# Softmax sums kept in one tile, range-checked in pieces, with a general version behind a branch

## The chip, the cores and the metric

The kernel runs on one core of a Trainium2 chip. The metric is the device time of one launch in microseconds (us), median of several runs. The core has five engines that work through queues of their own: TensorE (PE in the profile, its weight loads PEld), VectorE (DVE), ScalarE (ACT), GpSimd (POOL) and SyncE (SP), and 16 DMA engines.

## The reference

A dynamic convolution over 7 taps, whose weights are a softmax, followed by a two-layer network with the nonlinearity h - tanh(h). Shapes: x is 8 x 4096 x 192, weight_gen is 8 x 4096 x 8 heads x 7 taps, the two matrices are 192 x 2048 and 2048 x 192, all float32.

```python
def _attn_ref(x, weight_gen):
    B, S, D = x.shape
    H, K = (weight_gen.shape[2], weight_gen.shape[3])
    group = D // H
    w = weight_gen - np.max(weight_gen, axis=-1, keepdims=True)
    w = np.exp(w)
    w = w / (np.sum(w, axis=-1, keepdims=True) + 1e-09)
    pad = K - 1
    x_pad = np.concatenate([np.zeros((B, pad, D), dtype=np.float32), x], axis=1)
    idx = np.arange(S)[:, None] + np.arange(K)[None, :]
    x_unf = x_pad[:, idx, :].copy().reshape(B, S, K, H, group)
    return np.einsum('bshk,bskhg->bshg', w, x_unf).reshape(B, S, D)

def _moe_ref(x, w_in, w_out):
    h = x @ w_in
    g = h - np.tanh(h)
    return (g @ w_out).astype(np.float32)
```

The inputs of the softmax are normal numbers times 0.3. The reference subtracts the maximum of the 7 taps before the exponential.

## The kernel before

The 32768 tokens are cut into 32 blocks (n = 0 to 31) of 1024 tokens, 128 partitions with 8 tokens each. The whole loop over blocks is written out, and within `manual_schedule` (L564) the order of the Python calls is the order of the instructions in each engine's queue. No planner reorders them.

For a block the work is this. SP loads weight_gen (`load_wg`) and x with a halo of 6 rows (`load_x`). ScalarE takes the exponential in place (`softmax_exp`, L169), without subtracting a maximum. VectorE sums over the 7 taps (`softmax_sum`, L183, two halves of 128x224 elements to 128x32 in most blocks, into a tile `zsum` from a pool), takes the reciprocal (`softmax_norm`, L198, written to a corner of a PSUM tile) and scales (L229). GpSimd multiplies x by the weights, tap by tap (`products`, L299); transfers that add (L236) and transposing matmuls into one PSUM tile (`conv_sums`, L384) sum the taps; ScalarE copies the result to SBUF as bf16 (`conv_out`, L410). VectorE does the first two taps of one or two tokens of some blocks in a step of another block (`help`, L250 and L251).

The network runs in 16 steps f of 128 hidden units. `gemm1(n, f)` (L427) multiplies into a PSUM tile `ph` of 128x1024 float32, six matmuls; ScalarE takes tanh (L440), VectorE subtracts and writes a bf16 tile `gt` (L441). The second matmul (L495) is written as a stream of pairs, `out_pairs(m)`, that are laid between the steps: while block n runs its 16 steps, the pairs belong to block n-1, and a table (`STEADY` for the late blocks: 5, 11, 0, 16, 4, 12, ... pairs behind step 0, 1, 2, ...) says how many stand behind which step. The last pair of each group of 16 reads the `gt` of step 15. For block 31 the second matmul is done at the end, in `gemm2_last` (L538, L551, L552, L554): matmul, copy on ScalarE, add on VectorE, and a store on SP for every two of eight parts.

The tiles `ph` and the PSUM tiles of the transposes come from one pool, `psum_h`, with three buffers. So a step's matmul waits until the subtraction of the tile three places earlier has read it. The transposes for the next block stand behind steps 13 and 14 (`t2`, `t1`); block 31 has none. Where there is a later softmax, its reciprocal and scaling come behind step 14 (`softmax_norm`, "scale"). Blocks 28 to 31 have no later softmax: `soft` names block n+4 and is empty there.

The loop of blocks, with the places that the change touches:

```python
    for n in range(1, NTOT):
        ...
        soft = [m for m in (n + 3 if n <= AHEAD else n + 4,) if m < NTOT]
        for f in range(NFT):
            ph = gemm1(n, f)
            ...
            if n > 1:
                for h, at in enumerate(plan["sums"]):
                    if soft and f == at:
                        softmax_sum(soft[0], h * JH, (h + 1) * JH)
```

At the program's end each engine jumps to a last block, SP waits for all transfers, and all engines meet at two barriers, between which GpSimd clears the semaphores (all of it on line L800).

Of the kernel before, what the change touches and what calls it, by code (L numbers as in the profile page):

```python
# [8 lines left out]
FP32 = mybir.dt.float32  # L9
BF16 = mybir.dt.bfloat16  # L10

ACT = mybir.ActivationFunctionType
AX = mybir.AxisListType


@with_exitstack
def kernel(
# [8 lines left out]
    nc = tc.nc  # L26

    B, S, D = x.shape
    H, K = weight_gen.shape[2], weight_gen.shape[3]
    G = D // H  # L30
    F = moe_w_in.shape[1]
    P = nc.NUM_PARTITIONS
    R = P // 2
    HALO = K - 1

    J = 8
    TOK = P * J
    JH = J // 2
    HT = TOK // 2
    NSB = S // TOK  # L40
    NTOT = B * NSB
    NFT = F // P
    NC = D // R
# [7 lines left out]
    HELP = {n: ((n - 2, 3),) for n in (4, 5, 6, 7, 8, 9, 10, 11, 12, 13, 14, 15, 16, 17, 18, 19, 20, 21, 22, 23, 24, 25, 26, 27, 28, 29, 30, 31)} | {9: ((7, 3), (6, 12)), 10: ((8, 3), (7, 12)), 11: ((9, 3), (8, 12)), 12: ((10, 3), (9, 12)), 13: ((11, 3), (10, 12)), 14: ((12, 3), (11, 12))}  # L51
    LAST_TAP = (4, 5, 6, 7, 8)
    X_LATE = ()
    ZERO_AT = 8
    PACE, PACED = None, ()
    SCALE_TWICE = True
# [24 lines left out]
    zero = const.tile([1, D], FP32, name="zero")  # L81
    nc.vector.memzero(zero[:])
    once = const.tile([P, 1], FP32, name="once")

    x_of = {}
    held = {}
# [2 lines left out]
    zsum_of = {}  # L89
    zr_of = {}  # L90
    wsm_of = {}
    prods_of = {}
    to_sum = {}
    conv_of = {}
    g_of = {}
# [71 lines left out]
    def softmax_exp(n):  # L167
        wg_t = wg_of.pop(n)
        last_exp[0] = nc.scalar.activation(  # L169
            out=wg_t[:].rearrange("p j h k -> p (j h k)"),  # L170
            in_=wg_t[:].rearrange("p j h k -> p (j h k)"),
            func=ACT.Exp,
        )
        e_of[n] = wg_t
# [4 lines left out]
    def softmax_sum(n, j0=0, j1=J):  # L179

        if j0 == 0:
            zsum_of[n] = wgpool.tile([P, J * H], FP32, name="zsum")
        nc.vector.reduce_sum(  # L183
            out=zsum_of[n][:, j0 * H : j1 * H],
            in_=e_of[n][:, j0:j1].rearrange("p j h k -> p (j h) k"),
            axis=AX.X,
        )

    def softmax_recip(n, j0=0, j1=J):
        if j0 == 0:  # L190
# [3 lines left out]
    def softmax_norm(n, bank):  # L194

        wsm = softmax_tile()
        zr_v = bank[:, 512 - J * H : 512]
        nc.vector.reciprocal(zr_v, zsum_of[n][:])  # L198

        def finish():  # L200
            scale(nc.vector, wsm[:], e_of[n], zr_v)

        wsm_of[n] = (wsm, None, None, None)
        return finish

    def softmax_norm_ramp(n, bank):

        softmax_sum(n)
        wsm = softmax_tile()
        zr_v = bank[:, 512 - J * H : 512]  # L210
        nc.vector.reciprocal(zr_v, zsum_of[n][:])  # L211
        if n == 2:
            scale(nc.vector, wsm[:], e_of[n], zr_v)
            wsm_of[n] = (wsm, None, None, None)
            return
        wsm_v = bank[:, 0 : J * H * K].rearrange("p (j h k) -> p j h k", j=J, h=H)
        if n == 0 and SCALE_TWICE:
            scale(nc.vector, wsm[:], e_of[n], zr_v)
        ramp_scale[n] = scale(nc.vector, wsm_v, e_of[n], zr_v)
        if n == 1 or not SCALE_TWICE:  # L220
            nc.scalar.activation(  # L221
                out=wsm[:].rearrange("p j h k -> p (j h k)"),
                in_=wsm_v.rearrange("p j h k -> p (j h k)"),
                func=ACT.Copy,
            )
        wsm_of[n] = (wsm, wsm_v, None, None)
# [302 lines left out]
    def gemm2_last(j, f0=0, f1=NFT):  # L529

        n = NTOT - 1
        if f0 == 0:
            half[j] = psum_h.tile([P, 2, HT], FP32, name="po2", tag="ph")
        po = half[j]
        col = (j % 2) * HT + (j // 2) * P
        for f in range(f0, f1):
            for r in range(2):
                nc.tensor.matmul(  # L538
                    po[:, r, 0:D],
                    lhsT=g_of[n][f][r * R : (r + 1) * R, col : col + P],  # L540
                    rhs=w_out[r * R : (r + 1) * R, f, :],
                    start=(f == 0),
                    stop=(f == NFT - 1),
                )
# [15 lines left out]

    w_in = const.tile([P, NC, F], BF16, name="w_in")
    w_out = const.tile([P, NFT, D], BF16, name="w_out")

    ctx.enter_context(tc.manual_schedule())  # L564

    def load_w_out():
        nc.gpsimd.dma_start(out=w_out[:], in_=moe_w_out.rearrange("(c p) e -> p c e", c=NFT))
# [139 lines left out]
    for n in range(1, NTOT):  # L707
        more = n < NTOT - 1
        finish = []
        plan = FIRST if n == 1 else DOUBLE if n in DOUBLE_IN else APART if n in APART_IN else STEADY  # L710
# [4 lines that stand above are left out]
            if n == 1:  # L715
                if f == 1:
                    load_wg(5)
                if f == 5:
                    softmax_exp(4)
                steps = ((softmax_sum, 3), (softmax_recip, 3), (softmax_sum, 4))  # L720
                for at, (step, m, h) in zip(plan["sums"], [s + (h,) for s in steps for h in (0, 1)]):
                    if f == at:
                        step(m, h * JH, (h + 1) * JH)
                if f == 5:
                    wsm_of[3] = (softmax_tile(), None, e_of[3], zr_of[3])
                    rest = products(3)
            elif f == 1:
                if soft:
                    softmax_exp(soft[0])
                if n + 2 < NTOT:  # L730
                    rest = products(n + 2)
            if n == AHEAD and f == 4:
                softmax_exp(n + 4)
            if n > 1:
                for h, at in enumerate(plan["sums"]):
                    if soft and f == at:
                        softmax_sum(soft[0], h * JH, (h + 1) * JH)
            if n == AHEAD:
# [33 lines left out]
    gemm2_last(0, J, NFT)  # L772
    for j in range(1, J):
        gemm2_last(j)


# [28 lines left out]
```

## Time and profile before

| | |
|---|---|
| runs | 746.22 us median of 3 (744.88 to 746.73) |
| the profiled execution, span from first to last instruction | 743.4 us |
| TensorE busy | 722.3 us (97%) |
| VectorE busy | 687.4 us (92%) |
| ScalarE busy | 638.8 us (86%) |
| GpSimd busy | 654.5 us (88%) |
| L441, subtraction, 512 times | 601.6 us, 1217 ns each |
| L440, tanh, 512 times | 512.1 us, 1025 ns each |
| L183, sums, 61 times | 23.6 us |
| L198, reciprocals, 27 times | 14.9 us, 550 ns each |
| L229, scaling on VectorE, 27 times | 16.8 us, 621 ns each |
| granted TensorE clock | 0.995 of full |

Busy times are shares of one span in which the engines overlap. The span is that of one profiled execution; the runs' times cover what lies around it, too. In the prediction's extracts a timeline row has a start (us), a duration (us), the engine, the line, the operation with its result and its operands, a count, and in brackets the idle time before and what ended it. Rows that follow each other on an engine and are alike are put together, and their duration runs from the first start to the last end.

### The profile page before, as it was taken

To read this page: it belongs to the slowest core of one execution; us is meant where nothing else is said; L and a number is where in the kernel's file an instruction comes from. 1 tells how busy PE (TensorE), PEld (TensorE's weight loads), DVE (VectorE), ACT (ScalarE), POOL (GpSimd) and SP (SyncE) were. 2 spreads that over 40 slices of the span, in tenths; PEclk is the share of its full clock that TensorE was granted. 3 is DMA by queue.
4 is the path that set the end of the run, shared out by engine and by line. 5 is a ranking of instruction groups with operands and counts; after the bars stand their busy time and mean duration, and the time that the engine had idled before them with its cause. 6 is when DMAs were issued, how large, how long until landed. Compare 5 with 4: busy or idle time off the path is not lost.

```text
span 743.4 us, 30037 instructions
## 1 busy us (share of the span) xinstructions
PE 722.3 (97%) x13616; PEld 556.5 (75%) x13616; DVE 687.4 (92%) x723; ACT 638.8 (86%) x872; POOL 654.5 (88%) x163
## 2 busy tenths in 40 slices
PE   3899999999999999999999999999999999999997
PEld 2477777778777777777777777777777777877777
DVE  7999899999999999999999999999999999988893
ACT  4888888888888888989889999898998989888882
POOL 7999999999999999999999999999999999991000
PEclk9899999999999999999999999999999999999999
DMA  8925367766567668878777977877887877776112
GB/s 236 245 46 161 135 172 185 195 179 149 124 183 184 183 185 224 210 199 203 166 202 209 236 186 204 178 195 205 221 209 195 192 181 194 193 149 110 45 45 86
DMA packets 34269, 130.06 MB, mean 175 GB/s; under 512 B 4591, under 2 KB 9439, under 8 KB 30174
## 3 DMA queue, kind: packets, MB, share of 16 engines
q0 software_dynamic: 19424, 51.12, 40.4%
q1 hardware_dynamic: 14718, 77.03, 27.6%
q8 instruction: 106, 1.74, 0.9%
q14 instruction: 21, 0.17, 0.1%
HBM read 54.52 MB, written 25.17 MB: 107 GB/s over the span
## 4 chain that ended last, share of the span: by engine, by line
PE 92%; DVE 5%; ACT 1%; issue 1%; DMA 1%; SPq 0%; DVEq 0%
PE ph L427 43%; PE obank L495 43%; PE pc L384 4%; DVE gt L441 3%; PE po L538 1%; ACT th L440 1%; DVE pa L299 1%; DMA wg_t<-in_weight_gen_dram 1%; DVE zsum L183 0%; SPq L134 0%; ACT convT L402 0%; DVE obank L211 0%; DVE pa L251 0%; DVE pb L299 0%; SPq L144 0%
## 5 line engine op out<-in xcount | busy, mean ns | idle before, releaser
L441 DVE TENSOR_TENSOR gt<-ph,th 128x1024 bf16<-128x1024 f32 x512 | 601.6, 1217 | 33.4 <-ACT th L440 23.2
L440 ACT ACTIVATE th<-ph 128x1024 f32<-128x1024 f32 x512 | 512.1, 1025 | 69.2 <-PE ph L427 60.3
L427 PE MATMUL ph<-convT,w_in 64*128 64x512 bf16 x3072 | 415.1, 379 | 5.3 <-DVE gt L441 3.3
L495 PEld LDWEIGHTS <-gt 64*128 64x128 bf16 x7936 | 355.6, 94 | 80.6 <-issue 6.3
L495 PE MATMUL obank<-w_out,gt 64*128 64x192 bf16 x7936 | 408.0, 243 | 0.9 <-issue 0.8
L299 POOL TENSOR_TENSOR pa<-x_t,wsm 128x2688 bf16<-128x2688 f32 (+3 forms) x68 | 338.9, 5232 | 0.2
L299 POOL TENSOR_TENSOR pb<-x_t,wsm 128x4608 bf16<-128x4608 f32 (+2 forms) x33 | 283.8, 8601 | 0.7 <-ACT wsm L221 0.5
L427 PEld LDWEIGHTS <-w_in 64*128 64x128 bf16 x3072 | 163.0, 94 | 86.0 <-issue 18.3
L514 ACT ACTIVATE out_sb<-obank 128x192 f32<-128x192 f32 x248 | 81.3, 328 | 11.2 <-PE obank L495 10.3
L410 ACT ACTIVATE convT<-pc 128x1024 bf16<-128x1024 f32 (+1 forms) x62 | 50.1, 810 | 2.9 <-PE pc L384 2.7
L236 POOL DMA_DIRECT2D pa<-pb x28 | 36.0, 1284 | 13.7 <-POOL pb L299 9.1
L384 PEld LDWEIGHTS <-pa 64*128 64x128 bf16 x2064 | 41.5, 100 | 6.8 <-DVE pa L299 1.1
L236 POOL DMA_DIRECT2D pa<-pa x21 | 34.7, 1651 | 9.6 <-DMA pa<-pb 8.9
L384 PE MATMUL pc<-ident,pa 64*128 64x64 bf16 x1968 | 41.2, 191 | 1.8 <-POOL pa L299 0.9
L183 DVE TENSOR_REDUCE zsum<-wg_t 128x32 f32<-128x224 f32 (+1 forms) x61 | 23.6, 387 | 2.9 <-ACT wg_t L169 2.9
L169 ACT ACTIVATE wg_t<-wg_t 128x448 f32<-128x448 f32 x32 | 18.2, 570 | 6.3 <-DMA wg_t<-in_weight_gen_dram 6.2
L251 DVE TENSOR_TENSOR pa<-x_t,ph 128x384 bf16<-128x384 f32 x34 | 18.8, 554 | 2.0 <-DVE ph L250 0.3
L229 DVE TENSOR_TENSOR wsm<-wg_t,pc 128x448 f32<-128x448 f32 x27 | 16.8, 621 | 2.5
L198 DVE RECIPROCAL pc<-zsum 128x64 f32<-128x64 f32 x27 | 14.9, 550 | 0.0
L384 PE MATMUL pc<-ident,pb 64*128 64x64 bf16 x216 | 4.9, 206 | 9.0 <-POOL pb L299 9.0
L384 PEld LDWEIGHTS <-pb 64*128 64x128 bf16 x288 | 6.3, 106 | 9.5 <-POOL pb L299 9.0
L538 PE MATMUL po<-w_out,gt 64*128 64x192 bf16 x256 | 11.2, 243 | 0.0
(27 smaller groups left out, 56.8 us busy)
## 6 DMA issues: line engine op xcount, KB each, us to landing
x_t<-in_x_dram SPq DMA_DIRECT2D x31, 1344.0 KB, 7.9
pa<-pb POOLq DMA_DIRECT2D x28, 1152.0 KB, 9.5
out_dram<-out_sb SPq DMA_DIRECT2D x31, 768.0 KB, 3.9
pa<-pa POOLq DMA_DIRECT2D x21, 768.0 KB, 7.2
wg_t<-in_weight_gen_dram SPq DMA_DIRECT2D x32, 224.0 KB, 7.1
x_t<-in_x_dram SPq DMA_DIRECT2D x1, 768.0 KB
w_out<-in_moe_w_out_dram POOLq DMA_DIRECT2D x1, 768.0 KB, 9.5
out_dram<-out_sb SPq DMA_DIRECT2D x4, 192.0 KB, 3.0
```

The source lines that it names most:

```text
L183: nc.vector.reduce_sum(out=zsum_of[n][:, j0 * H : j1 * H], in_=e_of[n][:, j0:j1].rearrange("p j h k -> p (j h) k"), axis=AX.X,)
L236: return nc.gpsimd.dma_start(out=out.rearrange("p k j d -> p k (j d)"), in_=in_.rearrange("p k j d -> p k (j d)"), accum_op=mybir.AluOpTyp ...
L251: nc.vector.tensor_mul(pa[:, 0:KH, j, :].rearrange("p k (h g) -> p k h g", h=H), bass.AP(tensor=x_v.tensor, offset=x_v.offset + j * D, ap= ...
L299: return eng.tensor_mul(prod(k0, k1)[:, :, j0:j1].rearrange("p k j (h g) -> p k (j h) g", h=H), bass.AP(tensor=x_v.tensor, offset=x_v.offs ...
L384: nc.tensor.matmul(pc[r][:, col : col + R] if home else pc[:, r, col : col + R], lhsT=prods[c][gi][r * R : (r + 1) * R, 2 * j : 2 * j + 2] ...
L410: last_conv[0] = nc.scalar.activation(out=out, in_=pc[:, :, 0:cols].rearrange("p r (cj t) -> p r cj t", t=R), func=ACT.Copy,)
L427: nc.tensor.matmul(ph[:, r, :], lhsT=w_in[r * R : (r + 1) * R, c, f * P : (f + 1) * P], rhs=convT[r * R : (r + 1) * R, c, :], start=(c == ...
L440: last_act[0] = nc.scalar.activation(out=th[:], in_=ph_f, func=ACT.Tanh)
L441: last_sub[0] = nc.vector.tensor_sub(gt[:], ph_f, th[:])
L495: mm = nc.tensor.matmul(po[:, 0:D], lhsT=g_of[n][f][r * R : (r + 1) * R, col : col + P], rhs=w_out[r * R : (r + 1) * R, f, :], start=(r == ...
L514: last_act[0] = nc.scalar.activation(out=out_sb[:, j, :], in_=po[:, 0:D], func=ACT.Copy)
L538: nc.tensor.matmul(po[:, r, 0:D], lhsT=g_of[n][f][r * R : (r + 1) * R, col : col + P], rhs=w_out[r * R : (r + 1) * R, f, :], start=(f == 0 ...
```

## The change

The sums of exponentials of all 32 blocks go into one tile `zall` (128 x 2048) in place of a rotating tile per block. Eight pieces, at fixed places in the last four blocks, check that all sums lie between 1e-18 and 1e30: pieces 0 and 1 take the maximum over each half of `zall` per partition, 2 and 3 the minimum, 4 and 5 compare with the bounds, 6 multiplies the results and sends 128 x 2 numbers as one row to one partition through SP's queue, and 7 takes the minimum of that row into an integer `flag`. Behind the last block every engine reads `flag` into a register (`values_load`) and branches. If a sum was out of range, a loop over the 8 batches computes everything anew with the row maximum subtracted (`general`); otherwise that code is jumped over.

In the built program, up to the branch, each engine's instructions stand in the order of before, with the new ones between. SP's read of `flag` stands behind the transfer of the row and ahead of the last store of block 30 and the four stores of block 31. SP has four register moves more ahead of the first barrier. The engines' last block holds, for SP, a wait for each of the semaphores of transfers and engines; the way past the general version has some waits and updates of semaphores of its own. TensorE's part of the loop's body has 3,011 instructions, that of ScalarE 211, of VectorE 180, of SP some fifty.

```diff
@@ constants
+    SUM_MAX, SUM_MIN = 1e30, 1e-18
+    CHECK = {(28, 14): (0,), (29, 14): (1,), (30, 14): (2,), (31, 4): (3,), (31, 6): (4, 5, 6), (31, 13): (7,)}
@@ tiles
+    zall = const.tile([P, NTOT * J * H], FP32, name="zall")
+    ends = const.tile([P, 4], FP32, name="ends")
+    fine = const.tile([P, 2], FP32, name="fine")
+    fine_row = const.tile([1, 2 * P], FP32, name="fine_row")
+    flag = const.tile([1, 1], mybir.dt.int32, name="flag")
@@ softmax_sum
-            zsum_of[n] = wgpool.tile([P, J * H], FP32, name="zsum")
+            zsum_of[n] = zall[:, n * J * H : (n + 1) * J * H]
@@
+    def sums_piece(i):
+
+        w = NTOT * J * H // 2
+        if i < 4:
+            op = ALU.max if i < 2 else ALU.min
+            nc.vector.tensor_reduce(ends[:, i : i + 1], zall[:, i % 2 * w : (i % 2 + 1) * w], AX.X, op)
+        elif i == 4:
+            nc.vector.tensor_scalar(ends[:, 0:2], ends[:, 0:2], SUM_MAX, None, op0=ALU.is_le)
+        elif i == 5:
+            nc.vector.tensor_scalar(ends[:, 2:4], ends[:, 2:4], SUM_MIN, None, op0=ALU.is_ge)
+        elif i == 6:
+            nc.vector.tensor_mul(fine[:], ends[:, 0:2], ends[:, 2:4])
+            nc.sync.dma_start(out=fine_row[:], in_=fine[:])
+        else:
+            nc.vector.tensor_reduce(flag[:], fine_row[:], AX.X, ALU.min)
@@ softmax_norm, softmax_norm_ramp
-        nc.vector.reciprocal(zr_v, zsum_of[n][:])
+        nc.vector.reciprocal(zr_v, zsum_of[n])
@@
-    ctx.enter_context(tc.manual_schedule())
+    sched = tc.manual_schedule()
+    sched.__enter__()
@@ the loop of blocks, behind gemm1 and the loads of a step
+            for piece in CHECK.get((n, f), ()):
+                sums_piece(piece)
@@ the end
     for j in range(1, J):
         gemm2_last(j)
+    sched.__exit__(None, None, None)
+
+    def general(b, s):
+        ...
+        nc.vector.tensor_reduce(zr[:], e_v, AX.X, ALU.max)
+        nc.vector.tensor_sub(e_v, e_v, spread(zr[:]))
+        nc.scalar.activation(
+            out=e_t[:].rearrange("p j h k -> p (j h k)"),
+            in_=e_t[:].rearrange("p j h k -> p (j h k)"),
+            func=ACT.Exp,
+        )
+        ...
+
+    good = nc.values_load(flag[:], min_val=0, max_val=1)
+    with tc.If(good < 1, preferred_fallthrough_block=False):
+        with tc.For_i(0, B) as b:
+            for s in range(NSB):
+                general(b, s)
+            for s in range(NSB):
+                g_of.pop(NTOT + s)
+                conv_of.pop(NTOT + s)
```

More of the change, by code (lines that the diff above doesn't have):

```diff
@@ L13 @@
 AX = mybir.AxisListType
+ALU = mybir.AluOpType
 @with_exitstack
@@ L210, in softmax_norm_ramp @@
         zr_v = bank[:, 512 - J * H : 512]
-        nc.vector.reciprocal(zr_v, zsum_of[n][:])
+        nc.vector.reciprocal(zr_v, zsum_of[n])
         if n == 2:
@@ L774, with rows, spread @@
         gemm2_last(j)
+    sched.__exit__(None, None, None)
+    def general(b, s):
+        n = NTOT + s
+        s0 = s * TOK
+        x_t = xpool.tile([P, HALO + J, D], FP32, name="x_t")
+        def rows(p0, p1, r0, r1):
+            batch = x[bass.ds(b, 1)]
+            nc.sync.dma_start(
+                out=x_t[p0:p1, r0:r1, :],
+                in_=bass.AP(
+                    tensor=batch.tensor,
+                    offset=batch.offset + (s0 + p0 * J - HALO + r0) * D,
+                    ap=[[J * D, p1 - p0], [D, r1 - r0], [1, D]],
+                ),
+            )
+        if s == 0:
+            rows(0, P, HALO, HALO + J)
+            rows(1, P, 0, HALO)
+            nc.vector.memset(x_t[0:1, 0:HALO, :], 0.0)
+        else:
+            rows(0, P, 0, HALO + J)
+        e_t = wgpool.tile([P, J, H, K], FP32, name="wg_t")
+        nc.sync.dma_start(
+            out=e_t[:],
+            in_=weight_gen[bass.ds(b, 1), s0 : s0 + TOK].rearrange("o (p j) h k -> p (o j) h k", p=P),
+        )
+        e_v = e_t[:].rearrange("p j h k -> p (j h) k")
+        zr = wgpool.tile([P, J * H], FP32, name="zr")
+        def spread(v):
+            return v.rearrange("p (n o) -> p n o", o=1).to_broadcast([P, J * H, K])
+        nc.vector.tensor_reduce(zr[:], e_v, AX.X, ALU.max)
[4 more added lines that the diff above has]
+            func=ACT.Exp,
+        )
+        nc.vector.reduce_sum(out=zr[:], in_=e_v, axis=AX.X)
+        nc.vector.reciprocal(zr[:], zr[:])
+        nc.vector.tensor_mul(e_v, e_v, spread(zr[:]))
+        total = opool.tile([P, J, D], FP32, name="out_sb")
+        part = opool.tile([P, J, D], FP32, name="out_sb")
+        summed = pbpool.tile([P, J, D], BF16, name="pb")
+        x_v = x_t[:]
+        for k in range(K):
+            to = total if k == 0 else part
+            nc.vector.tensor_mul(
+                to[:].rearrange("p j (h g) -> p (j h) g", h=H),
+                bass.AP(tensor=x_v.tensor, offset=x_v.offset + k * D, ap=[x_v.ap[0], [G, J * H], [1, G]]),
+                e_t[:].rearrange("p j h (k o) -> p k (j h) o", o=1)[:, k].to_broadcast([P, J * H, G]),
+            )
+            if k > 0:
+                nc.vector.tensor_add((summed if k == K - 1 else total)[:], total[:], part[:])
+        prods_of[n] = [[summed[:]]] * NC
+        conv(n, (0, 1), (2,))
+        for f in range(NFT):
+            gemm1(n, f)
+        out_sb = opool.tile([P, J, D], FP32, name="out_sb")
+        for j in range(J):
+            po = psum_h.tile([P, 2, HT], FP32, name="po2", tag="ph")
+            col = (j % 2) * HT + (j // 2) * P
+            for f in range(NFT):
+                for r in range(2):
+                    nc.tensor.matmul(
+                        po[:, r, 0:D],
+                        lhsT=g_of[n][f][r * R : (r + 1) * R, col : col + P],
+                        rhs=w_out[r * R : (r + 1) * R, f, :],
+                        start=(f == 0),
+                        stop=(f == NFT - 1),
+                    )
+            ot = tpool.tile([P, D], FP32, name="ot", tag="th")
+            nc.scalar.activation(out=ot[:], in_=po[:, 0, 0:D], func=ACT.Copy)
+            nc.vector.tensor_add(out_sb[:, j, :], po[:, 1, 0:D], ot[:])
+        nc.sync.dma_start(
+            out=out.rearrange("(b s p j) e -> b s p j e", b=B, s=NSB, p=P)[bass.ds(b, 1), s].rearrange(
+                "o p j e -> p (o j) e"
+            ),
+            in_=out_sb[:],
+        )
```

## The prediction

> **What bounds the kernel now.** I read the share of each engine first, then the chain of work that ended last, then the timelines of VectorE and TensorE in the blocks where the new instructions stand, and last the instructions of the program's end.
>
> ```profile
> PE 722.3 (97%) x13616; PEld 556.5 (75%) x13616; DVE 687.4 (92%) x723; ACT 638.8 (86%) x872; POOL 654.5 (88%) x163
> ...
> PE 92%; DVE 5%; ACT 1%; issue 1%; DMA 1%; SPq 0%; DVEq 0%
> ```
>
> TensorE (PE) is busy for 97% of the span and makes 92% of the chain. VectorE (DVE) is close behind, so extra VectorE work costs time only where it makes TensorE wait. It does so through the ring of three PSUM tiles (psum_h): step f may write its tile only when the subtraction (L441) of the step three tiles earlier has ended.
>
> Blocks 27 and 28 on VectorE, around step 14 (start, duration, idle before in brackets):
>
> ```profile
> 640.01 0.55 DVE L198 RECIPROCAL pc<-zsum 128x64 f32<-128x64 f32 x1
> 640.66 0.62 DVE L229 TENSOR_TENSOR wsm<-wg_t,pc 128x448 f32<-128x448 f32 x1
> 641.20 3.67 DVE L441 TENSOR_TENSOR gt<-ph,th 128x1024 bf16<-128x1024 f32 x3
> ...
> 660.85 1.22 DVE L441 TENSOR_TENSOR gt<-ph,th 128x1024 bf16<-128x1024 f32 x1 [0.69 <-ACT th L440]
> 662.47 1.23 DVE L441 TENSOR_TENSOR gt<-ph,th 128x1024 bf16<-128x1024 f32 x1 [0.40 <-ACT th L440]
> 664.35 2.36 DVE L441 TENSOR_TENSOR gt<-ph,th 128x1024 bf16<-128x1024 f32 x2 [0.66 <-PE ph L427]
> ```
>
> Block 27 has a reciprocal and a scaling between the subtractions of steps 14 and 15; block 28 has none (there is no later softmax), and VectorE idles 0.40 and 0.66 us there. Now block 31. Its subtractions come in the groups f0-1, f2-3, f4-5 (at 713.26), f6-7 (715.87) and f8 to f13 (718.49); the first matmuls of TensorE below are those of f8 and f9, then f10 and f11 alone:
>
> ```profile
> 713.26 2.36 DVE L441 TENSOR_TENSOR gt<-ph,th 128x1024 bf16<-128x1024 f32 x2 [0.26 <-ACT th L440]
> 715.87 2.37 DVE L441 TENSOR_TENSOR gt<-ph,th 128x1024 bf16<-128x1024 f32 x2 [0.26 <-ACT th L440]
> 718.49 7.18 DVE L441 TENSOR_TENSOR gt<-ph,th 128x1024 bf16<-128x1024 f32 x6 [0.25 <-ACT th L440]
> ```
>
> ```profile
> 716.57 1.48 PE L427 MATMUL ph<-convT,w_in 64*128 64x512 bf16 x12
> 717.86 0.68 PE L495 MATMUL obank<-w_out,gt 64*128 64x192 bf16 x12
> 718.36 0.83 PE L427 MATMUL ph<-convT,w_in 64*128 64x512 bf16 x6
> ...
> 719.83 0.83 PE L427 MATMUL ph<-convT,w_in 64*128 64x512 bf16 x6
> ```
>
> What the reader is to see: the ring is tight here. Step 9 starts at 716.57 + 0.65 = 717.22 (six matmuls follow the next six by 0.65 us in the chain) and needs the subtraction of f6, which ends at 715.87 + 1.22 = 717.09: 0.13 us to spare. Step 10 starts at 718.36 and needs f7, which ends at 718.24: 0.12 us to spare. Step 8 (716.57) needs f5 (715.62): 0.95 us.
>
> Last, the prices of VectorE reductions, and the program's end (duration ns min/median/max, first and last start):
>
> ```profile
> L183 DVE TENSOR_REDUCE zsum<-wg_t 128x32 f32<-128x224 f32 x58 | 21.8, 375 | 0.0
> ...
> L183 DVE TENSOR_REDUCE zsum<-wg_t 128x64 f32<-128x448 f32 x3 | 1.8, 614 | 2.9 <-ACT wg_t L169 2.9
> ```
>
> ```profile
> L800 SPq EVENT_SEMAPHORE  x11: 17/28/28, 740.7 to 743.3; - x11
> ...
> L800 PEldq DRAIN  x2: 13/554/1095, 738.5 to 742.8; - x2
> ...
> L800 DVEq DRAIN  x2: 19/207/395, 740.0 to 742.8; - x2
> ```
>
> The last add on VectorE ends at 739.97 + 0.36 = 740.33; SP starts the last store there, it lands by 742.5, and two barriers fill the rest to 743.4. PE (done at 739.6), ScalarE (739.9) and VectorE (740.3) therefore sit 2.9, 2.6 and 2.2 us in front of the barrier.
>
> **The change, part by part.**
>
> Sums in one tile: the 61 reductions and the reciprocals keep shape, number, engine and place in the built program's order; only their tile differs. Nothing is removed and no wait is added. Cost 0; nothing needs to hide it.
>
> The four large reductions (pieces 0 to 3), each 128x1024: from 375 ns for 224 and 614 ns for 448 elements the slope is 1.067 ns an element and the rest 136 ns, so 1024 elements take 1.23 us (estimate from these two rows). Lower bound, if one run of 1024 reads twice as fast as groups of 7: about 0.68; upper bound: 1.75, the L299 row of a 128x1536 product on VectorE.
>
> Pieces 0, 1, 2 come behind step 14 of blocks 28, 29, 30. In block 28 the subtraction of f14 ends at 662.07, that of f15 moves from 662.47 to 663.30 and ends at 664.52, that of the next f0 moves from 664.35 to 664.52, and f2 is on time. The tile of f15 is wanted by the next block's f2 (665.02 + 0.65 = 665.67), 1.1 us later. The bf16 tile of f15 is wanted by the last pair of step 1, near 664.94: 0.4 us to spare. Cost 0. The cover is the idle 0.40 + 0.66 us plus the ring; block 27 carries 1.17 us at the same place without a wait of TensorE. Without cover it would be 3 x 1.23 = 3.7 us.
>
> Pieces 3 to 6 in block 31 are another matter. Subtractions follow each other by 1.15 us (two in 2.36). Piece 3 starts behind f4 at 714.40 and ends at 715.63; f5 ends at 716.85, so step 8 waits from 716.57 to 716.9. f6 starts at 716.78 and ends at 718.00, so step 9 starts at 718.06 instead of 717.22. Pieces 4, 5, 6 are three operations on 128x2 elements. Nearest row: the copy of 16 elements (L250) at 190 ns, with its follower 0.23 us after its start; I take 0.2 us each, 0.6 in all (0.3 if they overlap, 1.0 at the 342 ns of a 32-element reciprocal). They put f7 at 718.53 to 719.75, and step 10 starts at 719.81 instead of 718.36: **1.45 us** late. f8 then ends at 720.9 and step 11, due at 719.83 + 1.45 = 721.28, no longer waits. TensorE is the bound from there to 739.6, so nothing is won back. With the bounds: 0.68 + 0.3 gives about 0.6; 1.75 + 1.0 gives about 2.4.
>
> The row transfer (piece 6, on SP's queue) starts near 718.6. Behind it on SP stand the read of the flag, then the stores of block 30 and 31. Piece 7, which waits for the landing, is due behind f13, about 725.9 + 1.2 = 727.1, so 8.4 us are there; the x loads, hundreds of times larger, land after 8.4 us at most. Piece 7 itself (256 elements: 0.41 us) moves f14 and f15 by less than half a microsecond; f15 ends near 729.9, and the last block's second matmul wants it behind 730.2 + 1.45. SP reads the flag near 727.5, its next store waits for ScalarE until 730.07 + 1.45. Cost 0; if the landing were later than 8.4 us, VectorE would pass the excess on.
>
> The end. Each engine reads the flag, compares, runs one more wait and jumps over the general version. SP's part lies behind the last landing: about 12 further waits at 28 ns, 0.34 us, and a jump; at the program's start a barrier and a jump together take 0.29 us (last memset to first kernel instruction, 0.45 to 0.74). So 0.65 us, or 0.4 if the jump costs next to nothing. The other engines' reads and jumps lie in their 2.2 to 2.9 us. The trace shows no register read and no far jump. Bounds: nothing, if all is hidden; above, a read like a small store (2.1 us from issue to landing) and an instruction page. The instruction queue q8 moved 106 packets in 0.9% of 16 engines' 743.4 us, 1.0 us a packet of 16 KB. VectorE would then arrive at 740.33 + 2.1 + 0.29 + 1.0 = 743.7 against SP's 743.15, 0.55 us late; a whole 3.0 us (a store's median to landing) behind SP's own jump is the extreme. I take **0.5 us**, nearest to the first of these. End: 1.15 us, between 0.4 and 3.7.
>
> The Trainium skill speaks against the branch: "Runtime: NRT & Kernel Launch", Instruction fetch mechanics, says that a taken branch to a target outside the window of two pages stalls for a fetch by DMA. Only TensorE's jump (3,011 instructions in the loop's body, far over a page) is of that sort, and it has 2.9 us of cover. "DMA: Bandwidth & Descriptors", Latency and other measured facts, puts a register load near 0.6 us; by that page the 0.5 us would vanish and the sum would be 748.3 us. No row here shows either.
>
> Four register moves at SP's start lie in its wait for the first barrier (0.0 to 0.7 us): 0, or 0.11 uncovered.
>
> **Sum.** 1.45 + 1.15 = 2.6 us on the profiled 743.4 us, 746.0. The runs' median lies 2.8 us above the profiled span, in what surrounds the program and is not changed: 746.22 + 2.6 = **748.8 us**.
>
> **The rivals.**
>
> A, not slower by anything measurable: the end is free. All reads and jumps vanish in the wait for the last store, and SP pays only its 0.4 us. For it: 2.2 us of cover on the latest engine. Against: SP's jump is behind everything. 746.22 + 1.45 + 0.4 = 748.1. It decides when the end costs under 0.8 us.
>
> B, the check costs less: reductions at 0.68 us and small operations at 0.1 us. 746.22 + 0.6 + 1.15 = 748.0. For it: the fold is one long run. Against: both L183 rows fit one slope.
>
> C, a page is missing where nothing hides it, on SP or on two engines in turn: 3.0 us more than the 0.65. 746.22 + 1.45 + 3.65 = 751.3. For it: targets lie behind code that is never run. Against: SP's jump spans about a hundred instructions, less than one 16 KB packet of 256.
>
> D, the branch is taken, and the second version runs, at least another 700 us. The sums are those of 7 exponentials of values of order 0.3, near 7; only a fault would do it.
>
> **How the numbers follow.** This kernel's runs spread from 744.88 to 746.73, so 0.3% (2.2 us, 744.0 to 748.5) is what a measurement can tell from no change. Forecast 0.50, A 0.23, B 0.13, C 0.13, D below 0.01. The forecast's own range, 747.9 to 749.8, has a quarter inside the band; A and B lie in it for the most part, C above. That gives slower 0.57, same 0.40 and, for the spread alone, faster 0.03. Range: from A and B without part of the check, 746.9, to C, 751.4.
>
> **What would show it.** Right: in block 31 waits of TensorE (L427 for the subtraction) of about 0.3, 0.5 and 0.6 us at steps 8, 9, 10, none in 28 to 30, reductions of 1.23 us, TensorE's last matmul 1.45 us later against its first, and 1.15 us more from the last add to the span's end. Wrong: no wait at step 10, a wait for the row transfer, or an end longer by over 2 us.

## The result and the profile after

The changed kernel takes 749.49 us (median of 4 runs, 748.69 to 750.33), the kernel before in the same series 746.48 us (744.88 to 747.03). The ratio is 1.0048, 95% interval 1.0032 to 1.0063: slower by 3.0 us. The profiled execution spans 746.8 us, 3.4 us more than that of before. Of 77 runs of all kernels with the branch not taken, in the result and the experiments, six took 754.7 to 758.1 us, for a reason not known, and none of 122 runs without it took over 749; the six are in the ratios below but hardly move the medians, which are therefore compared.

The page of the changed kernel, engines and chain:

```profile
PE 722.3 (97%) x13616; PEld 555.4 (74%) x13616; DVE 692.4 (93%) x731; ACT 639.2 (86%) x872; POOL 654.7 (88%) x163
...
PE 91%; DVE 6%; DMA 1%; ACT 1%; issue 1%; SPq 0%; DVEq 0%
```

TensorE's busy time is the same 722.3 us. VectorE has 5.0 us more, and one percent of the chain has gone over to it. Where it did, the chain of waits in order of time tells (start, duration, what; changed kernel, block 31):

```profile
713.58 1.23 DVE gt L465
714.80 1.12 DVE ends L202
715.93 2.26 DVE gt L465 x2
718.19 0.07 DVE ends L204
718.27 0.08 DVE ends L206
718.35 0.02 issue
718.37 0.16 DVE fine L208
718.53 1.15 DVE gt L465
719.68 0.04 issue
719.72 0.82 PE ph L451 x6
...
```

From the subtraction of step 4 to that of step 7 the chain runs through VectorE, with piece 3 (L202) and the three small pieces (L204 to L208) in it, and returns to TensorE at step 10. TensorE's timeline shows the same from its side:

```profile
717.12 0.82 PE L451 MATMUL ph<-convT,w_in 64*128 64x512 bf16 x6
718.25 0.82 PE L451 MATMUL ph<-convT,w_in 64*128 64x512 bf16 x6 [0.31 <-DVE gt L465]
718.89 0.67 PE L519 MATMUL obank<-w_out,gt 64*128 64x192 bf16 x12
719.72 0.82 PE L451 MATMUL ph<-convT,w_in 64*128 64x512 bf16 x6 [0.16 <-DVE gt L465]
```

These are steps 8, 9 and 10. Step 0 of this block starts at 706.43 us, against 706.11 before; measured from there, step 8 is 0.23 us late, step 9 0.71 (718.25 - 717.22 - 0.32, with the prediction's 717.22), step 10 1.04 (719.72 - 718.36 - 0.32), and the last add 1.00 us. The bracketed idle time is less than the delay, since a matmul's modelled end reaches into the wait.

The other part is the end. Before, the span ended 743.4 - 740.33 = 3.07 us behind the last add; now the last add ends at 741.29 + 0.36 = 741.65 and the span 5.15 us later. The rows of the branch (L891) and of the closing block (L923), durations in ns, then first and last start:

```profile
L891 SPq EVENT_SEMAPHORE  x8: 17/17/17, 742.1 to 744.9; - x8
...
L891 PEldq COMPARE_BRANCH  x2: 95/1806/3518, 740.5 to 741.1; - x2
L891 ACTq COMPARE_BRANCH  x2: 38/41/44, 741.5 to 741.6; - x2
L891 DVEq COMPARE_BRANCH  x2: 51/53/55, 741.9 to 742.1; - x2
L891 SPq COMPARE_BRANCH  x2: 41/47/53, 742.0 to 745.0; - x2
```

```profile
L923 SPq EVENT_SEMAPHORE  x14: 17/28/28, 745.2 to 746.8; - x14
...
L923 SPq DRAIN  x3: 7/7/7, 745.9 to 746.3; - x3
L923 PEldq DRAIN  x2: 8/40/73, 744.7 to 746.3; - x2
L923 ACTq DRAIN  x2: 8/38/67, 744.9 to 746.3; - x2
L923 DVEq DRAIN  x2: 10/25/40, 745.5 to 746.3; - x2
```

TensorE's jump lasts 3.5 us, but TensorE is at the barrier (its DRAIN) by 744.7, ahead of SP at 745.9. The jumps of ScalarE and VectorE seem short, 0.04 and 0.05 us, but the next instruction of each, its DRAIN, starts 3.3 us behind the jump, at 744.9 and 745.5. So VectorE is only 0.5 us ahead of SP.

SP is the last. It issues the last store at 741.67 and waits for the landing in the way past the general version. The trace records the landing of a transfer in 16 signals, as many as there are DMA engines; the last of this store's comes at 744.83, 3.15 us behind the issue, against 742.21 - 740.36 = 1.85 before. Then SP ends the way past, jumps, runs its list of waits and is at the barrier 1.1 us behind the landing (745.95), against 0.24 before (742.45). So 1.3 us for the landing and 0.9 us for SP, less 0.1 us at the barriers, make the end's 2.1; with the 1.0 us in block 31 that is 3.1, for the 3.0 of the medians.

What of the landing? The DMA share in 40 equal slices (0.08 us in the first fence, 0.13 us in the second; the upper line in tenths) and the speed in GB/s, from the last add to the end; first the kernel before, then the changed one:

```profile
DMA  0000000000038999986000000000000000000000
GB/s 0 0 0 0 0 0 0 0 0 0 0 139 317 436 337 396 357 317 218 20 0 0 0 0 0 0 0 0 0 0 0 0 0 0 0 0 0 0 0 0
```

```profile
DMA  0005000999721222010000000000602000200000
GB/s 0 0 0 126 0 0 0 347 354 366 272 59 63 35 12 87 12 35 12 35 12 0 0 0 0 0 0 0 126 0 63 0 0 0 63 0 0 0 0 0
...
q8 instruction: 2, 0.03, 3.0%
q14 instruction: 5, 0.04, 3.0%
```

Before, the store's 192 KB move in 0.7 us. Now the bulk moves in 0.65 us too, but a tail of slices at 12 to 87 GB/s follows for 1.2 us, and seven packets of the instruction queues (16 KB and 8 KB) lie in a stretch that had none. Four of them start between the store's issue and the end of its data, one of 16 KB and three of 8 KB; the first starts at 742.03, 0.95 us behind the start of TensorE's jump. Not the whole store is late: 13 of its 16 signals come within 1.83 us of the issue, as before, and three at 2.40, 2.83 and 3.15.

That packets do this, with or without a jump, can be seen earlier in block 31, in the traces of all 13 kernels of this text whose general version is not run, that of before among them. Beside the second of the block's four stores a 16 KB packet moves, ahead of TensorE's branch: the last signal comes 2.7 to 3.6 us behind the issue, the other 15 by 1.88. Beside the third moves no packet, and all 16 signals come within 1.86. (The first overlaps with the store of block 30 and is left out.) Together with the last stores, one to three signals are late (behind 1.9 us) in all 21 stores with a packet beside them and none in the 18 without. On which DMA engine a packet moved, the trace does not record.

### The profile page after: what moved, and what is told of

Its sections match the earlier page's. It is cut to its first block, busy times and chain, and to the rows that moved or that the text cites. A ratio compares the mean times of both kernels' runs of the same rounds, so it can differ in the third digit from the quotient of the medians.

```text
span 746.8 us, 30082 instructions
## 1 busy us (share of the span) xinstructions
PE 722.3 (97%) x13616; PEld 555.4 (74%) x13616; DVE 692.4 (93%) x731; ACT 639.2 (86%) x872; POOL 654.7 (88%) x163
## 4 chain that ended last, share of the span: by engine, by line
PE 91%; DVE 6%; DMA 1%; ACT 1%; issue 1%; SPq 0%; DVEq 0%
PE ph L451 43%; PE obank L519 42%; PE pc L408 4%; DVE gt L465 4%; PE po L562 1%; DMA x_t<-zero 1%; DVE pa L323 1%; ACT th L464 1%; DVE zall L191 0%; PE obank L408 0%; SPq L142 0%; DVE obank L235 0%; DVE pa L275 0%; DVE ends L202 0%; DVE pb L323 0%
## 5 line engine op out<-in xcount | busy, mean ns | idle before, releaser
L191 DVE TENSOR_REDUCE zall<-wg_t 128x32 f32<-128x224 f32 (+1 forms) x61 | 23.7, 388 | 3.0 <-ACT wg_t L177 3.0
L222 DVE RECIPROCAL pc<-zall 128x64 f32<-128x64 f32 x27 | 14.9, 550 | 0.0
```

The costliest lines, as they stand in the source:

```text
L191: nc.vector.reduce_sum(out=zsum_of[n][:, j0 * H : j1 * H], in_=e_of[n][:, j0:j1].rearrange("p j h k -> p (j h) k"), axis=AX.X,)
```

## The experiments

The theory was: two separate costs, a ring stall of TensorE in block 31 and a longer end, in which SP's jump and waits behind the landing, and instruction packets beside the last store, have a part each. The "before" of each series is its own: 745.95 us for the first four, 745.89 for the next four, 745.97 for the ninth to eleventh, 746.13 for the last. An end is the time from the end of the last add to the end of the span (3.07 us before); a landing is the last of the 16 signals, counted from the store's issue.

**The check alone.** The branch is taken out; the flag is written for nobody.

```diff
-    good = nc.values_load(flag[:], min_val=0, max_val=1)
-    with tc.If(good < 1, preferred_fallthrough_block=False):
-        ...
```

> The eight pieces of the check alone; the flag is written and nobody reads it, no branch and no general version. Theory (ring stall in block 31 plus a longer end, two separate costs): TensorE waits for the subtraction at steps 9 and 10 of block 31 and is 1.0 us late from there on; from the last add to the end of the span it is 3.1 us as before; time about 1.0 us over the kernel before. Rival 1 (all of the loss is at the end, the check is hidden): equal to before within 0.3 us. Rival 2 (the check is all of it): 3.0 us over before.

747.14 us, 1.2 over before; ratio 1.0019 (1.0010 to 1.0028). Step 10 is again 1.04 us late against the block's first steps, with the same two waits; the span ends 3.3 us behind the last add, 0.2 more than before; the landing, 1.82 us, has no part in that, and its cause was not looked for. Both rivals fall.

**The branch alone.**

```diff
-    CHECK = {(28, 14): (0,), (29, 14): (1,), (30, 14): (2,), (31, 4): (3,), (31, 6): (4, 5, 6), (31, 13): (7,)}
+    CHECK = {(31, 13): (7,)}
@@ sums_piece
-            nc.vector.tensor_reduce(flag[:], fine_row[:], AX.X, ALU.min)
+            nc.vector.memset(flag[:], 1)
```

> No check: the flag is set to 1 by one small VectorE instruction behind step 13 of block 31; the reads of the flag, the branch and the whole general version stay. Left out: the range check. Theory: no wait of TensorE in block 31; from the last add to the end of the span 5.1 us, against 3.1; time about 2.1 us over before. Rival 1 (the end costs nothing lasting, its 2.1 us in one trace was chance): within 0.5 us of before. Rival 2 (the branch is all of the loss): 3.0 us over before.

747.95 us, 2.0 over before; ratio 1.0048 (1.0018 to 1.0078). No wait of TensorE for a subtraction in block 31, 5.1 us from the last add to the end, landing 3.0 us. Both rivals fall here, too. The two parts add up: 1.2 + 2.0 = 3.2 for the 3.0 measured.

**A near branch.** As before, and

```diff
-            for s in range(NSB):
-                general(b, s)
+            general(b, 0)
...
@@ general
-        for f in range(NFT):
+        for f in range(1):
             gemm1(n, f)
...
-        for j in range(J):
+        for j in range(1):
...
-            for f in range(NFT):
+            for f in range(1):
```

> As the branch alone, but the general version is cut to one block, one step and one eighth of the output, so that TensorE jumps over some 70 instructions in place of 3,000. Left out: the range check and most of the general version, which is never run. Theory (the far jump fetches instruction pages on the same DMA engines as the last store, whose landing moves from 2.1 to about 3.1 us behind its issue): the compare-and-branch entry of TensorE falls from 3.5 us to under 0.5, the last store lands 2.1 us behind its issue again, and the time from last add to the end falls from 5.1 to about 4.1 us, 1.0 us over before. Rival (SP's chain of waits and its own jump behind the landing is the cost, the landing is late for another reason): 5.1 us from the last add to the end as with the whole version, 2.1 us over before.

747.40 us, 1.45 over before; ratio 1.0017 (1.0008 to 1.0026). TensorE's jump takes 0.33 us and the end 3.9 us, as the theory said, but not for its reason: the landing is still late, 2.75 us, and one instruction packet of each queue still lies beside the store. What was saved is SP's part. With fewer transfers in the general version, the way past it raises only four of the eight semaphores of SP's transfers, the last store's not among them, so SP's jump (742.6) and most of its waits (from 742.8) come ahead of the landing (744.2), and SP is at the barrier 0.2 us behind it. ScalarE and VectorE, which jump over less code here, go on 0.13 and 0.16 us behind their jumps.

**The sums alone.**

```diff
-    CHECK = {(28, 14): (0,), ...}
+    CHECK = {}
```

The branch is out as well.

> Only the sums go into one tile; no check, no reads, no branch. Theory: within 0.3 us of before. Rival (the place of the sums in memory, or the way the tile's dependences are kept, has a price of its own): over 0.5 us more than before, spread over the blocks.

745.91 us, 0.04 under before; ratio 0.9998 (0.9990 to 1.0007). The place of the sums costs nothing.

**The check later.** Without the branch:

```diff
-    CHECK = {..., (30, 14): (2,), (31, 4): (3,), (31, 6): (4, 5, 6), (31, 13): (7,)}
+    CHECK = {..., (30, 14): (2,), (31, 15): (3, 4, 5, 6)}
@@
     for j in range(1, J):
         gemm2_last(j)
+        if j == 2:
+            sums_piece(7)
```

> The check alone, no branch, as in the first experiment, but pieces 3 to 6 stand behind the last subtraction (step 15 of block 31), where VectorE waits 2.2 us for the last matmuls, and piece 7 behind the third of the eight last adds. Left out: the reads of the flag, the branch and the general version. Theory (the loss of the check is the ring of three PSUM tiles at steps 8 to 10 of block 31): TensorE waits for no subtraction in block 31, the time falls from 1.2 us over before to within 0.4 us. Rival (more work on VectorE costs wherever it stands, as its 92% suggest): still 1.2 us over before.

746.25 us, 0.36 over before; ratio 1.0003 (0.9992 to 1.0013). Pieces 0 to 2 stand where they stood; pieces 3 to 7 now stand in VectorE's idle time (its timeline here; the second row's bracket is what is left of 2.2 us):

```profile
731.31 0.16 DVE L208 TENSOR_TENSOR fine<-ends 128x2 f32<-128x2 f32 x1
732.20 0.36 DVE L576 TENSOR_TENSOR out_sb<-po,ot 128x192 f32<-128x192 f32 x1 [0.72 <-ACT ot L575]
```

TensorE waits for no subtraction in block 31. The ring is the cause of the 1.0 us in that block, not the amount of work. Of the 0.36 us left, 0.2 are the longer end (3.3 us) that the check alone had, too.

**Late check and branch.** The whole change, with these places, and the reads of the flag inside the order written by hand, behind the last store.

```diff
+    good = nc.values_load(flag[:], min_val=0, max_val=1)
     sched.__exit__(None, None, None)
...
-    good = nc.values_load(flag[:], min_val=0, max_val=1)
```

> The whole change (check, branch and general version), with the pieces as late as in the experiment before and each engine's read of the flag as its last instruction ahead of the branch, SP's behind its last store. Theory: no wait of TensorE in block 31, the end as long as in the changed kernel (5.1 to 5.3 us from the last add); about 2.1 us over before, 1.0 under the changed kernel. Rival (SP's read of the flag behind the last store lengthens the end by its 0.5 us and more): 2.8 us or more over before.

748.25 us, 2.4 over before; ratio 1.0028 (1.0018 to 1.0038). TensorE waits for no subtraction in block 31, and the end takes 5.3 us. The time lies between theory (2.1) and rival (2.8), nearer the theory, and is what the check later and the branch alone add up to (0.36 + 2.0). Against the changed kernel 0.65 us are won, not the 1.0 expected.

**One block in the general version**, and **TensorE alone far**. In the first, `general(b, 0)` stands in place of the four calls, uncut; in the second, the near branch's one step of the last matmul is repeated:

```diff
-            for f in range(1):
+            for f in range(720):
                 for r in range(2):
                     nc.tensor.matmul(
```

> The branch alone with a general version of one block of a batch in place of four, so that TensorE jumps over some 750 instructions (48 KB at 64 bytes each), the other engines over 14 to 55. Left out: the check and three quarters of the general version, which is never run. Theory (a far jump of TensorE fetches pages): if 48 KB are already far, the compare-and-branch entry is 3.3 us and the end 4.6 us or more; if near, it is 0.3 us and the end 3.9 us, as with 70 instructions. Rival (the instructions' number does not matter, the other engines' jumps do): end 3.9 us with a compare-and-branch entry of 3.3 us.

> The near branch of the third experiment, with TensorE's part of the code behind the branch made long again (2,900 instructions of repeated matmuls, never run), all other engines' parts as short as there. Left out: the check and the general version. Theory (TensorE's far jump and its pages delay the last store): compare-and-branch entry 3.3 us or more, instruction packets in the stretch of the last store, its landing near 3 us behind its issue; end 4.6 to 5.1 us, and the time as in the branch alone, 0.6 us or more over the near branch. Rival (the other engines' pages and SP's longer list of waits make the difference between 3.9 and 5.1 us): end 3.9 us.

747.80 and 747.54 us, 1.9 and 1.65 over before; ratios 1.0040 (1.0015 to 1.0066) and 1.0044 (1.0020 to 1.0068). TensorE's jump takes 3.3 us over 750 instructions and 3.8 over 2,900, so 48 KB are far. The ends take 4.0 and 4.25 us, the landings 2.9 and 3.1. The seventh run comes close to its rival's numbers (3.3 and 3.9); the eighth lies between its two (4.6 or more, and 3.9), and its time only 0.2 us over the near branch, not the 0.6 that the theory gave. So TensorE's far jump lengthens the end by 0.1 to 0.4 us against the near branch. The rest of the whole branch's 5.1 us is mostly SP's part: it is at the barrier 1.2 us behind the landing there (second run) and 0.2 in these.

**A later last store.** The changed kernel with two idle reductions ahead of the last add:

```diff
     for j in range(1, J):
+        if j == J - 1:
+            for _ in range(2):
+                nc.vector.tensor_reduce(idle[:], zall[:, 0:1024], AX.X, ALU.max)
         gemm2_last(j)
```

> The changed kernel, whole, with two more reductions of 128x1024 on VectorE ahead of the last add of all, whose results nobody reads; the last add and the last store move by about 1.3 us against TensorE's jump. Theory (the last store lands late because instruction packets, fetched after the jump, lie on the same DMA engines while its data moves): the store's data now move behind the first instruction packet, the landing comes 2.1 us behind its issue, and from the last add to the end it is 4.1 us in place of 5.1; the time grows by only 0.3 us over the changed kernel, 3.3 over before. Rival (the landing is late whenever the code has the branch, whatever moves beside it): 5.1 us from the last add, 1.3 us over the changed kernel, 4.3 over before.

750.34 us, 4.4 over before; ratio 1.0060 (1.0046 to 1.0073), 5.0 us from the last add: the rival's numbers. TensorE's first packet ends 0.5 us behind the store's issue, before its data move (from 0.8), but the packets of the other engines, whose jumps follow the last add, do not: three of 8 KB start while the data move. One of the 16 signals is late, at 2.96 us; the other 15 come by 1.86. So the theory's forecast was wrong, but the run does not decide for the rival, since packets still lay beside the store.

**The general version's transfers on GpSimd.** On top of the late check and branch:

```diff
@@ general
-        nc.sync.dma_start(
+        nc.gpsimd.dma_start(
```

at its three places.

> As the whole change with the late pieces, and the transfers of the general version issued from GpSimd in place of SP, so that none of the semaphores of SP's transfers has to be raised on the way past it, and SP need not wait for the last landing ahead of its jump. Theory (about 1.0 us of the end is SP's jump and its twelve waits, which stand behind the landing only because the way past the general version waits for the last store first): SP's jump comes ahead of the landing, from the last add to the end 4.0 to 4.3 us, time about 1.2 us over before and 1.0 under the version with the late pieces alone. Rival (the landing alone makes the end longer; SP's jump is cheap): 5.1 us and no gain.

747.19 us, 1.2 over before; ratio 1.0029 (1.0007 to 1.0050). SP's rows, way past (L893) and closing block (L925):

```profile
L893 SPq COMPARE_BRANCH  x2: 38/46/53, 741.5 to 741.6; - x2
```

```profile
L925 SPq EVENT_SEMAPHORE  x14: 17/28/28, 742.2 to 744.7; - x14
...
L925 SPq DRAIN  x3: 7/7/13, 743.6 to 744.1; - x3
...
L925 DVEq DRAIN  x2: 10/25/40, 743.9 to 744.2; - x2
```

The jump lies at 741.6, two microseconds ahead of the drain at 743.6, and no wait stands between jump and list. The rival falls. The end takes 4.5 us, against 5.3 in the sixth run, with a landing of 3.2 (3.3 there). It is 0.2 more than expected: now VectorE, whose DRAIN starts at 743.87, 3.15 us behind its jump, comes to the barrier behind SP (743.65). The version is 1.1 us below the sixth run's by the two medians' distances from before, of which the end explains 0.8, and some 1.8 below the changed kernel's distance; it does not beat the kernel before.

**The branch taken.** The same with `SUM_MIN` at 1000, so that the flag is 0.

> The kernel before this one with the lower bound of the sums set to 1000, so that the check fails and the general version runs behind the whole kernel: what the branch costs when it is taken, which the prediction bounded by 700 us more. Per block a serial chain of loads (8 us), softmax (some 3 us), 13 passes of 1.75 us on VectorE, the transposes, 16 steps at no less than 1.4 us and eight output parts; 45 to 60 us a block with little overlap, 1450 to 1900 us for the 32, so 2200 to 2700 us in all. The other theories have no say in it.

2808.55 us (one run), above the expected 2200 to 2700: the general version costs 2,060 us, 64 us a block. TensorE is busy 56% of the span, VectorE 78%.

**The flag last.** As the late check and branch, with the row transfer behind the last store and the flag behind the last add:

```diff
             nc.vector.tensor_mul(fine[:], ends[:, 0:2], ends[:, 2:4])
-            nc.sync.dma_start(out=fine_row[:], in_=fine[:])
         else:
+            nc.sync.dma_start(out=fine_row[:], in_=fine[:])
             nc.vector.tensor_reduce(flag[:], fine_row[:], AX.X, ALU.min)
@@
     for j in range(1, J):
         gemm2_last(j)
-        if j == 2:
-            sums_piece(7)
+    sums_piece(7)
```

> The whole change with the late pieces, but the row transfer issued behind the last store and the flag's reduction behind the last add, so that every engine's read of the flag and jump come after the last store's data have moved. Theory (instruction packets fetched around the jumps spread the last store's data over 1.5 us and more and so delay its landing): the store's data move within 0.8 us as before the change, without a tail of slices at 12 to 40 GB/s, and the instruction packets come behind them. Rival (the tail belongs to the code's length or to the state of the chip, not to the jumps): the tail is there although no jump has been made. In either case the chain flag, read, TensorE's jump (0.4 + 0.5 + 3.4 us) now stands behind the landings: from the last add to the end 8 to 9.5 us, some 6 us over before.

750.72 us (one run, before 746.13), 4.6 over before where some 6 were expected; the end, 8.3 us, is within the expected 8 to 9.5. The DMA speed, 740.5 to 745.0 us in 40 slices of 0.11 us:

```profile
GB/s 0 0 0 0 0 0 0 96 396 396 396 369 96 0 6 4 0 0 0 0 0 0 0 0 0 0 0 0 0 0 0 0 0 0 0 0 0 0 0 73
```

The store moves in 0.7 us without the tail (the 6 and 4 are the row transfer), and all its 16 signals come within 1.82 us. The instruction packets come at the very end, behind the reads of the flag (743.3 us) and the jumps (from 743.9). The code is as long as in the changed kernel. So the tail does not belong to the length of the code; it goes where the jumps and their packets go.

## Why the prediction held, point by point

The predicted 748.8 us stands 0.7 below the measured 749.49, and the range held it; slower by over 0.3% was the likeliest case and is what came. The sum of 2.6 us for 3.0 was made of one term too large (by 0.4) and one too small (by 1.0), so a part of the nearness is luck.

**Sums in one tile, 0:** shown by the fourth experiment.

**Pieces 0 to 2, 0:** right, no wait of TensorE. One number of the working was wrong: the tile of f15 is wanted by f2 at 665.02, not 665.67 (that is f3), so 0.5 us were to spare, not 1.1. It did not matter.

**Reductions of 1.23 us:** 1.21 measured, and 1.13 from start to start, since an instruction's end overlaps the next one's start by 0.08 us.

**Block 31, 1.45 us:** the mechanism was right, by the chain, the two waits and the fifth experiment; the size was 1.04. The terms that were mis-sized are the three small operations, taken at 0.6 us and measured at 0.34 (718.11 to 718.45; 0.16 busy each, but two of them overlap), and the 0.1 us of the large one. The predicted delays at steps 8, 9, 10 were 0.34, 0.84 and 1.45, the measured 0.23, 0.71 and 1.04.

**The row transfer, 0:** right. It starts at 718.6, and the flag's reduction at 726.90 waits for nothing.

**The end, 1.15 us:** measured 2.1, within the stated bounds of 0.4 to 3.7. Its first term, 0.65 us for SP behind the landing, was right in kind and small: 0.9 us more than before, because twelve waits take about 0.06 us each from start to start (745.17 to 745.95), not 0.028. Its second term, 0.5 us, was put in the wrong place. It was to be VectorE's read and page in front of the barrier. VectorE's read took 0.54 us, and the stall behind its jump, 3.3 us, is longer than the 1.0 us that the prediction gave a page; but SP was later still, by 0.5 us, and covered it. What stands in its place is the last store's landing, 1.3 us later. The prediction had counted the instruction packets as a wait of the engine that jumps, and not as traffic beside a transfer that everybody waits for.

**Rival A** (the end is free) and **B** (the check is cheap) are refuted: by the end of 2.1 us and the second experiment, and by reductions of 1.21 us and the first, though B's 0.1 us for a small operation was right (0.34 for three). **C** had the right place, SP behind the landing, but no page is missing there (its entry takes 0.04 us, and the next instruction starts 0.2 us behind the entry's start); where engines do stall, on TensorE, ScalarE and VectorE, SP covers it. **D** did not happen, and would have cost 2,060 us (eleventh experiment).

**The span and the median:** the 2.8 us between them were not a constant. In all four runs of the changed kernel the time lies 1.8 to 1.9 us above the same run's span (748.69 and 746.8, 750.33 and 748.5), and in all later runs of the kernel before 1.7 to 2.0, so the profiled execution of before was probably among the quicker of its series.

The Trainium skill ("Runtime: NRT & Kernel Launch", Instruction fetch mechanics) had it that a jump far ahead stalls for a fetch; TensorE's 3.3 to 3.8 us over 750 to 3,011 instructions, against 0.33 over 70, agree. The prediction took only TensorE's jump to be of that sort. ScalarE's and VectorE's, over the whole general version (loop bodies of 211 and 180 instructions), were too: they went on 3.1 to 3.3 us behind their jumps in the changed kernel and the second experiment, against 0.13 and 0.16 in the third. The stalls alone would not have told the time, since SP came later in the whole change. "DMA: Bandwidth & Descriptors" (Latency and other measured facts) gives a register load some 0.6 us; the reads took 0.46 to 0.54 here, and VectorE's next instruction started 0.62 us behind the start of its read.

**What stays open.** That instruction packets beside a store make a part of it late is shown by the twelfth experiment and by the signals of the 39 stores; that a packet holds up the share of the store that is to move on the same DMA engine is the simplest reading, and was not shown, since the trace does not tell the packets' engines. In the ninth experiment only 8 KB packets, behind the other engines' jumps, start while the store's data move, and one signal is still late; how many of the late signals of the changed kernel belong to which of its four packets was not found out.

## What to carry to other kernels

Work added to a nearly full engine costs by where it stands: the same check cost 1.2 us at two steps of a tight ring, and 0.4 us or nothing where the engine waited for the last matmuls. Before placing it, subtract, buffer by buffer, the time at which each slot is wanted from the time at which it comes free; the spare of 0.12 and 0.13 us told it here.

A branch at the end costs even when it is not taken, on the engine that waits for the last store: look at what stands behind that landing (waits that make up for the code passed over, the jump, the closing list), and keep the skipped code off that engine's semaphores. Code behind a branch is also traffic: the instruction packets that follow the jumps made one to three of the last store's 16 parts late here. And an engine can stall behind a jump whose own entry looks short, so look at when its next instruction starts: once SP was out of the way, VectorE's stall was the next to set the end.

## What the runs showed of the hardware that was not expected

- A compare-and-branch entry takes 0.037 to 0.055 us on SP, ScalarE, GpSimd and VectorE, even where the engine then stands still for 3.3 us (ScalarE and VectorE of the changed kernel); on TensorE the stall is in the entry. TensorE's jump over 48 KB takes as long (3.3 us) as one over 190 KB (3.3 to 3.8).
- One 16 KB instruction packet beside a store of 192 KB goes with one late landing signal of the store's 16, in 13 of 13 traces: it comes 2.7 to 3.6 us behind the issue, against 1.82 to 1.86 for the last one without a packet.
- The instruction queues move 16 KB packets for one queue (106 for the 1.74 MB of TensorE's stream) and 8 KB packets for the other.
- The same code drifts from execution to execution ahead of its end: with the sums alone changed the last add came at 741.35 us, before at 739.97, and the two kernels do not differ by their medians. Differences under 1.5 us must be read within a stretch, from a common start.
